# One pool of eight PSUM banks, and a table of offsets that sets the order of every step

## The chip, the cores and the metric

The kernel runs on one core of a Trainium2 chip. The core has five engines with instruction queues of their own: PE multiplies matrices, DVE, ACT and POOL work on vectors, and SP only issues DMA transfers. Each engine takes its instructions strictly in the order in which the program lists them, and waits on semaphores where an operand or a buffer is not ready. The metric is device time in microseconds, the median of several executions; less is better.

## The reference

Eight batches of attention with 8 heads of 64, 512 local and 32 global tokens, followed by a two-layer MoE block with one expert on all 4,352 tokens. Cut to what matters:

```
s_g   = scale * q_g @ concat(k_g, k_l).T          # 32 global queries see all 544 keys
s_l   = scale * q_l @ k_l.T, only |i - j| <= 32   # local queries see a band ...
s_lg  = scale * q_l @ k_g.T                       # ... and the 32 global keys
out   = softmax(...) @ concat(v_g, v_l)           # both kinds
x     = out as [4352, 512]
h     = x @ w_in                                  # 512 -> 2048
g     = h where h >= 1, 0 where h <= -1, (h + 1)^2 / 4 between
y     = g @ w_out                                 # 2048 -> 512
```

The attention inputs are float32; both weights are float64 and arrive as words of 64 bits.

## The kernel before

Every product is computed with operands that are split into two float16 halves (a high part and the rest), so one logical product is three matmuls that add up in PSUM: high by high, low by high, high by low.

**Weights** (`win_decode`, `win_scale`, `win_halves` and the same for `w_out`): a tile of 128 rows of float64 words is loaded; ACT takes the magnitude of the upper words, a shift of the lower words (DVE in all 32 tiles before) and two more DVE instructions (SCALAR_TENSOR_TENSOR) put 32-bit magnitudes and signs together; PE sums magnitudes for a scale per group of four tiles; then the tile is split into halves, in one of several ways (a string of three letters per tile names the engines; `e` goes through PE with a scaled identity `sid` in float32). There are 16 tiles of each weight.

**Attention** of batch b: `scale_k/q/v` find powers of two for the operands, `prep_k/q/v` split them, `turn` transposes a split tile of 128 by 1024 (eight blocks of 128 by 128). `att_a(b, i, pr)` handles a pair of heads for 128 queries: scores on PE, a masked maximum on DVE (the custom instruction that writes `tts_t`, and `small_nb` for the offset), exponentials on ACT (`pf`), the split of the probabilities (`pb`: the high half by a cast, the low half by a subtraction on POOL), and `turn` into `pt`. `att_b` multiplies with the values, `att_x` normalises, splits and transposes the result into `xt`. `glob_a/b` do the global queries.

**MoE** in slices of 256 tokens, called by step name `m<slice>.<f>` for the first layer (24 matmuls of 128x256; `moe1`) and `o<slice>.<tile><part>` for the second (12 of 128x512; `moe2`). After each first-layer group there are an ACT instruction, two DVE instructions of 128x512 (the ones that write `ps_h_h` and `moe_t_r`), an ACT cast and a POOL subtraction. Batch 0 gives slices 0 and 1, batch 1 gives slices 2 and 3, and so on.

**Transposes.** Before, all of batch 0 that goes through `turn` (10 tiles of k and q and 16 of probabilities) is transposed on PE with an identity, and ACT copies the PSUM tile out. Batches 1 to 7, and `xt` in all batches, go through a DMA transpose issued by SP.

**PSUM** has eight banks. Before they are four pools of fixed use: `ps_h` 3 (first layer, transposes, weight halves), `ps_o` 2 (second layer, weight sums), `ps_s` 2 (scores), `ps_x` 1 (attention output).

**What sets the order.** The program is recorded first, without being issued. `segments` groups the recorded instructions of a step by engine and finds which segment must follow which. `schedule` then plays the segments through with a table of costs (`cost`): at each moment each free engine takes, among the segments that are ready by that table and whose buffers are free, the one with the lowest `prio`. Buffers of one tag are given out nearly in recorded order: a tile may take a buffer only if the earliest tile without one keeps a free one and is less than the pool's size behind. Before, `prio` is a start time per step from the numbers in `T`; a second pass uses deadlines instead, and the better one of the two is issued. The instructions are then written out in that order, engine by engine, and nothing reorders them any more. In the profile all of them have one line (L1238), so tiles and not lines tell the steps apart.

Of the kernel before, what the change touches and what calls it, by code (L numbers as in the profile page):

```python
# [107 lines left out]

def free(ap):
    n = 1  # L110
    for d in ap.shape[1:]:
        n *= d
    return n


def cost(engine, op, a, k, outs, ins, tiles):
# [3 lines left out]
    if engine == "tensor":  # L120
        if ins and ins[0].dtype == F32:
            return 4 * n / 2.4 + 10, 0
        t = max(28.0, n / 2.4 + 2.5)
        return (t / 4 if o.shape[0] == 32 else t), 0
    if engine == "sync":
# [4 lines left out]
        return 560.0, b / (186.0 if run < 512 else 264.0 if run < 1024 else 280.0)  # L130
    if engine == "scalar":
        own = 90 if op != "activation" or mybir.dt.size(o.dtype) == 2 else 190 if "accum_out" in k else 235
# [15 lines left out]
class Segment:  # L148
    __slots__ = ("n", "engine", "calls", "t", "xfer", "after", "before", "new", "uses", "load", "step", "left", "ready", "prio", "t0", "done")


def segments(steps, tiles, prio, names):
# [5 lines left out]
    for sn, calls in enumerate(steps):  # L158
        cur = None
        for engine, op, a, k in calls:  # L160
# [3 lines left out]
            if cur is None or cur.engine != engine or engine == "sync" or fresh & {tiles[nm][0] for nm in cur.new}:  # L164
                cur = Segment()
                cur.n, cur.engine, cur.calls, cur.t, cur.xfer = len(segs), engine, [], 0.0, 0.0
# [4 lines left out]

            near = [x.tensor.name for x in sides(*cur.calls[-2])[0]] if len(cur.calls) > 1 else []
            cur.t += t + (100.0 if engine in ("vector", "scalar") and any(x.tensor.name in near for x in ins) else 0.0)
# [30 lines left out]
def schedule(segs, tiles, hop, slack, landing, ahead):  # L204
# [15 lines left out]
    for g in segs:  # L220
        if g.left == 0:
            waiting[g.engine].append(g)
    free_at = {e: 0.0 for e in engines}
    dma_free, now, events, order, landed = 0.0, 0.0, [], [], []
    while len(order) < len(segs) or events:
        went = True
        while went:
            went = False
            for e in engines:
# [3 lines left out]
                for g in waiting[e]:  # L233
                    if g.ready > now or (best is not None and (g.prio, g.n) > (best.prio, best.n)):
# [6 lines left out]
                    if any(len(slots[tag]) < len(x) + (min(x) > head[tag]) or max(x) - head[tag] >= many[tag] for tag, x in need.items()):  # L241
# [3 lines left out]
                    best = g  # L245
                if best is None:
# [3 lines left out]
                waiting[e].remove(g)  # L250
# [5 lines left out]
                free_at[e] = now + g.t  # L256
                done = now + g.t
# [17 lines left out]
        while events and events[0][0] <= now:  # L275
# [3 lines left out]
            for b in g.before:  # L279
                c = segs[b]  # L280
                wait = (hop if c.engine != g.engine else 60.0) + (slack if c.engine == "tensor" and g.engine != "tensor" else 0.0)
                c.ready = max(c.ready, now + wait)
                c.left -= 1
                if c.left == 0:
                    waiting[c.engine].append(c)
# [998 lines left out]
```

## Time and profile before

| what | us |
|---|---|
| median of 3 runs (987.35 to 989.39) | 988.6 |
| the profiled execution, its own time | 987.26 |
| its span, first to last instruction | 985.5 |
| PE busy | 904.5 |
| DVE busy | 730.4 |
| ACT busy | 601.0 |
| POOL busy | 359.5 |
| mean granted TensorE clock | 0.968 |

A busy engine in this table is one with an instruction under way; a matmul counts until its result is out, so a busy PE need not be at its peak. The span is shown in the page as 40 slices of 24.6 us, and it divides into two parts: the first quarter, in which weights are decoded while batches 0 and 1 are worked on, and the rest, in which PE is busy without a break.

### The profile page before, as it was taken

Reading aid. Unit: us, or ns where it says so; the run is one execution under the profiler, and the core shown is the slowest. Engines: PE = TensorE matmul, PEld = TensorE weight load, DVE = VectorE, ACT = ScalarE, POOL = GpSimd, SP = SyncE. Lnnn points to the kernel's source line nnn. Section 1 sums busy time; section 2 is a strip of 40 time slices with the busy share of each in tenths; the row PEclk is TensorE's granted clock in tenths of the full one; section 3 lists DMA queues with packets and bytes.
Section 4 is the critical chain, followed back from the end, with each engine's and each line's share of the span. In section 5 each row is a group of like instructions: output and inputs, shape, how many; then the busy total and the mean of one; then the engine's idle time right before and its main releaser. Section 6 shows DMA issues by size and latency. Waiting matters only on the chain.

```text
span 985.5 us, 24720 instructions
## 1 busy us (share of the span) xinstructions
PE 904.5 (92%) x9499; PEld 641.4 (65%) x9500; DVE 730.4 (74%) x1956; ACT 601.0 (61%) x1418; POOL 359.5 (36%) x383
## 2 busy tenths in 40 slices
PE   2676767898899999999999999999999999999998
PEld 1453543575667676767676777867776767676765
DVE  4799998698787879677964868787867796565432
ACT  7897768675757656656663656666676654444321
POOL 4134462254414434343433333433333343332211
PEclk9877977999899999999999999999999999999999
DMA  9842534778989659956892659766886685344101
GB/s 236 233 147 64 168 88 102 145 161 144 175 155 177 119 128 152 182 113 128 153 186 45 134 111 170 136 114 130 160 175 114 128 134 108 59 79 66 33 1 33
DMA packets 370102, 125.23 MB, mean 127 GB/s; under 512 B 346432, under 2 KB 355648, under 8 KB 369984
## 3 DMA queue, kind: packets, MB, share of 16 engines
q1 hardware_dynamic: 369984, 123.65, 63.4%
q8 instruction: 74, 1.21, 0.5%
q14 instruction: 44, 0.36, 0.1%
HBM read 43.52 MB, written 8.91 MB: 53 GB/s over the span
## 4 chain that ended last, share of the span: by engine, by line
PE 71%; DVE 16%; DMA 5%; issue 3%; ACT 2%; POOL 1%; SPq 1%; DVEq 0%; POOLq 0%; ACTq 0%
PE ps_h_h L1238 32%; PE ps_o_o L1238 30%; PE ps_s_s L1238 5%; PE ps_x_x L1238 5%; DVE tmp_tmp L1238 2%; DVE weights_w L1238 2%; DVE tts_t L1238 1%; DVE nat_nat L1238 1%; DMA xt_xt<-xn_xh 1%; DMA weights_w<-in_moe_w_in_dram 1%; DVE batch_small_ms L1238 1%; DVE ps_h_h L1238 1%; SPq L1238 1%; DVE moe_t_r L1238 1%; DVE batch_small_q L1238 1%
## 5 line engine op out<-in xcount | busy, mean ns | idle before, releaser
L1238 PE MATMUL ps_h_h<-xt_xt,weights_w 128*128 128x256 f16 (+1 forms) x3456 | 383.3, 270 | 10.2 <-ACT pt_pt L1238 6.0
L1238 PE MATMUL ps_o_o<-weights_w,hidden_g 128*128 128x512 f16 x1632 | 376.6, 381 | 2.8 <-DVE xt_xt L1238 2.8
L1238 PEld LDWEIGHTS <-weights_w 128*128 128x128 f16 x3456 | 321.7, 99 | 61.5 <-issue 15.5
L1238 PEld LDWEIGHTS <-hidden_g 128*128 128x128 f16 x1744 | 161.5, 100 | 177.6 <-issue 12.1
L1238 POOL TENSOR_TENSOR hidden_g<-moe_t_r,hidden_g 128x512 f16<-128x512 f32 (+1 forms) x144 | 165.6, 1150 | 273.2 <-ACT hidden_g L1238 267.2
L1238 POOL TENSOR_TENSOR const_pb<-pf_pf,const_pb 128x384 f16<-128x384 f32 (+1 forms) x124 | 129.3, 1045 | 276.9 <-DVE const_pb L1238 195.8
L1238 ACT ACTIVATE moe_t_r<-ps_h_h,batch_small_ms 128x512 f32<-128x512 f32 (+1 forms) x144 | 107.9, 749 | 127.2 <-PE ps_h_h L1238 119.3
L1238 DVE SCALAR_TENSOR_TENSOR ps_h_h<-ps_h_h,batch_small_ms,moe_t_r 128x512 f32<-128x512 f32 (+1 forms) x144 | 104.2, 723 | 93.0 <-ACT moe_t_r L1238 92.9
L1238 ACT ACTIVATE pf_pf<-tts_t,small_nb 128x224 f32<-128x224 f32 (+1 forms) x256 | 117.3, 459 | 91.2 <-DVE small_nb L1238 77.1
L1238 DVE CUSTOM_DVE_ANT_0 tts_t<-ps_s_s,const_mask,batch_small_q 128x192 f32<-128x192 f32 (+1 forms) x256 | 100.2, 427 | 41.1 <-PE ps_s_s L1238 39.0
L1238 ACT CAST hidden_g<-moe_t_r 128x512 f16<-128x512 f32 (+1 forms) x144 | 84.7, 588 | 61.0 <-DVE moe_t_r L1238 60.6
L1238 DVE SCALAR_TENSOR_TENSOR moe_t_r<-moe_t_r,batch_small_ms,ps_h_h 128x512 f32<-128x512 f32 (+1 forms) x144 | 103.4, 718 | 5.5
L1238 ACT ACTIVATE junk_junk<-stage_st 128x512 f16<-128x512 f32 (+1 forms) x108 | 67.5, 625 | 25.5 <-DMA stage_st<-in_v_l_dram 8.7
L1238 PE MATMUL ps_s_s<-kt_kt,qt_qa 128*128 128x32 f16 (+2 forms) x704 | 69.8, 199 | 10.4 <-DVE small_nb L1238 5.6
L1238 PEld LDWEIGHTS <-pt_pt 128*128 128x128 f16 (+1 forms) x1536 | 61.8, 98 | 15.4 <-ACT pt_pt L1238 2.5
L1238 PE MATMUL ps_x_x<-v_v,pt_pt 128*128 128x64 f16 (+1 forms) x1536 | 67.7, 194 | 0.8 <-DVE moe_t_r L1238 0.5
L1238 PE MATMUL ps_s_s<-kt_kt,qt_qb 128*128 128x32 f16 (+2 forms) x704 | 65.9, 198 | 0.0
L1238 PEld LDWEIGHTS <-qt_qb 128*128 128x128 f16 x704 | 55.4, 98 | 16.1 <-issue 13.1
L1238 PEld LDWEIGHTS <-qt_qa 128*128 128x128 f16 x704 | 59.4, 98 | 5.1 <-issue 1.5
L1238 DVE CAST const_pb<-pf_pf 128x384 f16<-128x384 f32 (+1 forms) x112 | 47.7, 431 | 10.7 <-DMA pt_pt<-const_pb 6.6
L1238 ACT ACTIVATION_READ_ACCUMULATOR pf_pf<-tts_t,small_nb 128x1 f32 x256 | 47.8, 187 | 0.0
L1238 DVE TENSOR_SCALAR small_nb<-small_nb 128x2 f32<-128x2 f32 x128 | 35.4, 277 | 4.4
(165 smaller groups left out, 900.5 us busy)
## 6 DMA issues: line engine op xcount, KB each, us to landing
stage_st<-in_q_l_dram SPq DMA_DIRECT2D x32, 256.0 KB, 4.2
weights_w<-in_moe_w_in_dram SPq DMA_DIRECT2D x32, 256.0 KB, 4.0
qt_qb<-qt_qa SPq DMA_DIRECT2D x64, 128.0 KB, 3.0
stage_st<-in_moe_w_out_dram SPq DMA_DIRECT2D x32, 256.0 KB, 3.3
out_dram<-tmp_tmp SPq DMA_DIRECT2D x30, 256.0 KB, 2.5
stage_st<-in_k_l_dram SPq DMA_DIRECT2D x24, 256.0 KB, 3.6
stage_st<-in_v_l_dram SPq DMA_DIRECT2D x21, 256.0 KB, 3.8
v_v<-v_v SPq DMA_DIRECT2D x16, 128.0 KB, 2.7
```

Source lines behind the costliest of these rows:

```text
L1238: getattr(getattr(tc.nc, engine), op)(*a, **k)
```

## The change

It has these parts.

1. **PSUM**: one pool `ps` of eight banks with one tag `b`; every PSUM tile takes any free bank. The rule on recorded order now runs over all PSUM tiles together, with a reach of eight.
2. **The planner**: `plan` makes one pass. `prio` is the deadline of a segment (`deadlines`, counted backwards over the recorded order), and to it is added an offset for the step from a new table `LATER` (323 entries, in microseconds). Segments are shorter: a chain on DVE or ACT in which one instruction reads what the one before wrote is now cut apart, so other work can be put between.
3. **The costs** of the planner: other figures for DMA, ACT and float32 matmuls; matmuls in the first 200 us cost 1.1 times as much; instructions for which `shares` holds (all of POOL but memsets, and DVE instructions with two tensors in SBUF, or a copy or tensor_scalar of SBUF) are played one after the other across the two engines.
4. **Who does what**, by strings in `T`: `turns` (batch 0's 16 probability tiles go through a DMA transpose instead of PE and ACT; k and q of batch 0 stay on PE), `shifts` (7 of 32 shifts go from DVE to POOL, where one shift is two instructions), `subs` (8 low halves of probabilities of batches 0 and 1 go from POOL to DVE), `glow` (4 low halves of slices 0 and 1 from POOL to DVE), `casts` (3 casts of batch 1 from DVE to ACT), `lows` (2 of batch 1's `att_x` subtractions from DVE to POOL), `adds` (3 of the `small_nb` additions to ACT, 3 cut in two), `splits`, `halves` (13 tiles instead of 12 go through PE's float32 identity).
5. Eight single-column maxima of `win_scale` are done as three by broadcasting.

```diff
+def shares(engine, op, a, k, tiles):
+    if engine == "gpsimd":
+        return op != "memset"
+    if engine != "vector" or op in ("memset", "reciprocal", "tensor_reduce", "tensor_tensor_reduce"):
+        return False
+    ins = {"tensor_scalar": a[1:2], "tensor_copy": a[1:2], "scalar_tensor_tensor": [a[1], a[3]] if len(a) > 3 else []}.get(op, a[1:3])
+    ins = list(ins) or [k["in0"], k["in1"]]
+    held = [x for x in ins if is_ap(x) and not tiles.get(x.tensor.name, (0, 0, 1))[2]]
+    return len(held) > 1 or (op in ("tensor_scalar", "tensor_copy") and len(held) == 1 and free(held[0]) > 1)
...
-                free_at[e] = now + g.t
-                done = now + g.t
+                done, slow = now, SLOW if e == "tensor" and now < 2.0e5 else 1.0
+                for t, shared in g.parts:
+                    if shared:
+                        pair = done = max(pair - LEAD, done) + t
+                    else:
+                        done += t * slow
+                free_at[e] = done
...
 def plan(steps, tiles, prio, names, hop, slack, landing, ahead):
     segs = segments(steps, tiles, prio, names)
-    best = None
-    for n in range(PASSES):
-        order, taken, end = schedule(segs, tiles, hop, slack, landing, ahead)
-        if best is None or end < best[2]:
-            best = order, taken, end, [g.t0 for g in segs]
-        deadlines(segs, [g.n for g in segs] if n == 0 else order, hop, slack, landing)
-    order, taken, end, t0 = best
-    for g, t in zip(segs, t0):
-        g.t0 = t
+    if T["late"]:
+        deadlines(segs, [g.n for g in segs], hop, slack, landing)
+    for g in segs:
+        g.prio += LATER.get(g.step, 0.0) * (1.0e3 if T["late"] else 1.0)
+    order, taken, _ = schedule(segs, tiles, hop, slack, landing, ahead)
     return order, segs, taken
...
-    ps_h = pool("ps_h", 3, space=PSUM)
-    ps_o = pool("ps_o", 2, space=PSUM)
-    ps_s = pool("ps_s", 2, space=PSUM)
-    ps_x = pool("ps_x", 1, space=PSUM)
+    ps = pool("ps", 8, space=PSUM)
...
-    def turn(b, o, i):
-        if b:
+    def turn(who, o, i):
+        if who == "d":
             dma_t(o, i)
             return
         n = i.shape[0]
-        t = ps_h.tile([P, 8, P], F16, tag="h", name="turn")
+        t = ps.tile([P, 8, P], F16, tag="b", name="turn")
         for c in range(8):
             nc.tensor.transpose(t[:, c, :n], i[:, c * P:(c + 1) * P], ident[:n, :n])
-        nc.scalar.copy(o, t[:, :, :n])
+        (nc.scalar.copy if who == "a" else nc.vector.tensor_copy)(o, t[:, :, :n])
...
-        (nc.vector.tensor_copy if b else nc.scalar.copy)(pb[:, 0, :, :w], pf[:, :, :w])
-        nc.gpsimd.tensor_tensor(pb[:, 1, :, :w], pf[:, :, :w], pb[:, 0, :, :w], op=ALU.subtract)
+        (nc.scalar.copy if of("casts", b, 4 * i + pr, 16, "v") == "a" else nc.vector.tensor_copy)(pb[:, 0, :, :w], pf[:, :, :w])
+        (nc.vector if of("subs", b, 4 * i + pr, 16, "p") == "v" else nc.gpsimd).tensor_tensor(pb[:, 1, :, :w], pf[:, :, :w], pb[:, 0, :, :w], op=ALU.subtract)
         pt = ptp.tile([P, 2, 2, 2, P], F16, tag="pt", name=f"pt{b}_{i}_{pr}")
-        turn(b, pt.rearrange("p j u c k -> p (j u c) k"), pb.rearrange("p j u c -> p (j u c)"))
+        turn(of("turns", b, 10 + 4 * i + pr, 30, "d"), pt.rearrange("p j u c k -> p (j u c) k"), pb.rearrange("p j u c -> p (j u c)"))
...
+LATER = {"Lk00": -3, "Lk01": -33.7, "Lk02": 1.2, "Lk10": -99.1, "Lk11": 66.5, "Lk12": 98.5, "Lk20": -95.5, "Lk21": -87.9,
...
+T = dict(late=1, lk0=1.06, lq0=1.76, lv0=30, sk=12, sq=14, adds="vvvvvv1vvvvvavvvvvvvavv1vvvvv1av",
+         subs="pppppppppppvvvpppppvpvpvvppppvpp", glow="pppvpppvpppvpvpp",
+         turns="aaaaaaaaaadddddddddddddddddddddddddddddddddddddddddddddddddd", casts="aaaaaaaaaaaaaaaavvavvvavvvvvvavv",
...
+         shifts="pppvpvvpvvvvvvvvvvvvvvvvvpvvvpvv", splits="vvvvvvvvvvvpvvvpvvvpvppp", att=1.35, s0=60, s1=100, s2=254.09,
```

Three places in the order show what moved.

**DVE, the first instructions.** Tiles `weights_w` are weight tiles, `tmp_tmp` their magnitudes, `small_amk` and `batch_small_q` the scales of k and q. Before:

```order
L1238 TENSOR_REDUCE small_amk_91<-small_amk_91 128x1
L1238 TENSOR_SCALAR small_asx_93<-small_amk_91 128x1
L1238 COPY small_amk_91<-ps_s_s_97 128x1
L1238 TENSOR_SCALAR small_amk_91<-small_amk_91 128x1 x2
L1238 TENSOR_SCALAR batch_small_sk_98<-small_amk_91 128x1
L1238 RECIPROCAL batch_small_sk_98<-batch_small_sk_98 128x1
L1238 TENSOR_SCALAR batch_small_q_0_102<-batch_small_q_0_102 128x2 x3
```

With the change:

```order
L1278 SCALAR_TENSOR_TENSOR tmp_tmp_90<-tmp_tmp_90,weights_w_0_66 128x512
L1278 SCALAR_TENSOR_TENSOR weights_w_0_66<-weights_w_0_66,tmp_tmp_90 128x512
L1278 SCALAR_TENSOR_TENSOR tmp_tmp_95<-tmp_tmp_95,weights_w_0_67 128x512
L1278 SCALAR_TENSOR_TENSOR weights_w_0_67<-weights_w_0_67,tmp_tmp_95 128x512
L1278 SCALAR_TENSOR_TENSOR tmp_tmp_96<-tmp_tmp_96,weights_w_0_68 128x512
L1278 TENSOR_SCALAR weights_w_0_69<-weights_w_0_69 128x512
L1278 SCALAR_TENSOR_TENSOR weights_w_0_68<-weights_w_0_68,tmp_tmp_96 128x512
```

The decoding of the first four weight tiles now stands ahead of the scales of k and q, and the shifts of the first three of them are on POOL.

**ACT before, SP with the change: the probability tiles of batch 0.** `pf` are exponentials, `hidden_g` and `const_pb` the split probabilities, `pt` their transposes. On ACT before:

```order
L1238 ACTIVATE pf_pf_139,small_sum_138<-tts_t_153,small_nb_152 128x192 x2
L1238 CAST hidden_g_140<-pf_pf_139 128x2x192
L1238 ACTIVATE hidden_g_109<-stage_st_116,batch_small_q_0_102 128x8x64
L1238 COPY pt_pt_147<-ps_h_h_105 128x1024
L1238 ACTIVATE pf_pf_146,small_sum_138<-tts_t_137,small_nb_136 128x192 x2
L1238 CAST hidden_g_141<-pf_pf_146 128x2x192
L1238 ACTIVATE tmp_tmp_120<-weights_w_0_72 128x512
L1238 COPY pt_pt_154<-ps_h_h_105 128x1024
```

On SP with the change, where before only loads and copies stood:

```order
L1280 DMA stage_st_87<-in_moe_w_out_dram 128x512 x2
L1278 DMA_TRANSPOSE pt_pt_135<-const_pb_0_61 128x8x128
L1278 DMA_TRANSPOSE pt_pt_144<-hidden_g_133 128x8x128
L1278 DMA_TRANSPOSE pt_pt_138<-const_pb_0_62 128x8x128
L1278 DMA v_v_0_156<-v_v_149 32x1024
L1278 DMA v_v_159<-v_v_149 32x1024
L1278 DMA v_v_1_158<-v_v_149 32x1024
L1280 DMA stage_st_126<-in_moe_w_out_dram 128x512 x2
```

The 16 ACT copies and the 128 PE transposes ahead of them are gone from their queues, and 16 transposes stand in SP's queue between loads of `w_out`.

**DVE, the passage from slice 0 to slice 1.** `xt_xt_89` and `xt_xt_139` hold the output of slice 0 here; a pair that writes a PSUM tile and then `moe_t_r` belongs to a first-layer group of slice 1. Before:

```order
L1238 SCALAR_TENSOR_TENSOR nat_nat_190<-stage_st_85,batch_small_sk_186,nat_nat_190 128x8x64
L1238 SCALAR_TENSOR_TENSOR xt_xt_89<-ps_o_o_115,batch_small_ms_170,xt_xt_89 128x512
L1238 SCALAR_TENSOR_TENSOR xt_xt_89<-ps_o_o_143,batch_small_ms_170,xt_xt_89 128x512
L1238 SCALAR_TENSOR_TENSOR xt_xt_89<-ps_o_o_115,batch_small_ms_170,xt_xt_89 128x512
L1238 SCALAR_TENSOR_TENSOR nat_nat_190<-stage_st_0_87,batch_small_sk_186,nat_nat_190 32x8x64
L1238 SCALAR_TENSOR_TENSOR nat_nat_192<-stage_st_86,batch_small_q_1_198,nat_nat_192 128x8x64
L1238 SCALAR_TENSOR_TENSOR ps_h_h_101<-ps_h_h_101,batch_small_ms_170,moe_t_r_171 128x512
L1238 SCALAR_TENSOR_TENSOR moe_t_r_171<-moe_t_r_171,batch_small_ms_170,ps_h_h_101 128x512
```

With the change:

```order
L1278 SCALAR_TENSOR_TENSOR ps_b_102<-ps_b_102,batch_small_ms_171,moe_t_r_173 128x512
L1278 SCALAR_TENSOR_TENSOR nat_nat_195<-stage_st_0_88,batch_small_sk_192,nat_nat_195 32x8x64
L1278 SCALAR_TENSOR_TENSOR moe_t_r_173<-moe_t_r_173,batch_small_ms_171,ps_b_102 128x512
L1278 SCALAR_TENSOR_TENSOR ps_b_94<-ps_b_94,batch_small_ms_171,moe_t_r_172 128x512
L1278 SCALAR_TENSOR_TENSOR moe_t_r_172<-moe_t_r_172,batch_small_ms_171,ps_b_94 128x512
L1278 SCALAR_TENSOR_TENSOR nat_nat_193<-stage_st_86,batch_small_q_1_199,nat_nat_193 128x8x64
L1278 SCALAR_TENSOR_TENSOR xt_xt_139<-ps_b_117,batch_small_ms_171,xt_xt_139 128x512
```

Before, slice 0 was finished on DVE before slice 1 began; now two groups of slice 1 stand ahead of slice 0's last parts.

More of the change, by code (lines that the diff above doesn't have):

```diff
@@ L148 @@
 class Segment:
-    __slots__ = ("n", "engine", "calls", "t", "xfer", "after", "before", "new", "uses", "load", "step", "left", "ready", "prio", "t0", "done")
+    __slots__ = ("n", "engine", "calls", "t", "xfer", "after", "before", "new", "uses", "load", "step", "parts", "left", "ready", "prio", "t0", "done")
 def segments(steps, tiles, prio, names):
@@ L170, in segments @@
             cur.calls.append((op, a, k))
-            near = [x.tensor.name for x in sides(*cur.calls[-2])[0]] if len(cur.calls) > 1 else []
-            cur.t += t + (100.0 if engine in ("vector", "scalar") and any(x.tensor.name in near for x in ins) else 0.0)
+            cur.t += t
+            cur.parts.append((t, shares(engine, op, a, k, tiles)))
             cur.xfer += x
@@ L221, in schedule @@
         if g.left == 0:
-            waiting[g.engine].append(g)
+            bisect.insort(waiting[g.engine], (g.prio, g.n, g))
     free_at = {e: 0.0 for e in engines}
-    dma_free, now, events, order, landed = 0.0, 0.0, [], [], []
+    dma_free, pair, now, events, order, landed = 0.0, 0.0, 0.0, [], [], []
     while len(order) < len(segs) or events:
@@ L232, in schedule @@
                 best = None
-                for g in waiting[e]:
-                    if g.ready > now or (best is not None and (g.prio, g.n) > (best.prio, best.n)):
+                for at, (_, _, g) in enumerate(waiting[e]):
+                    if g.ready > now:
                         continue
@@ L280, in schedule @@
                 c = segs[b]
-                wait = (hop if c.engine != g.engine else 60.0) + (slack if c.engine == "tensor" and g.engine != "tensor" else 0.0)
+                wait = (hop if c.engine != g.engine else OWN) + (slack if c.engine == "tensor" and g.engine != "tensor" else 0.0)
                 c.ready = max(c.ready, now + wait)
@@ L302, in deadlines @@
             c = segs[b]
-            wait = (hop if c.engine != g.engine else 60.0) + (slack if c.engine == "tensor" and g.engine != "tensor" else 0.0)
+            wait = (hop if c.engine != g.engine else OWN) + (slack if c.engine == "tensor" and g.engine != "tensor" else 0.0)
             x = min(x, late[b] - wait - took)
@@ L858, in att_a @@
                                            op0=ALU.add, op1=ALU.min, accum_out=nb[:, u:u + 1])
[L859 removed]
+        who = of("adds", b, 4 * i + pr, 16, "v")
+        if who == "a":
+            nc.scalar.activation(nb2, nb, AF.Identity, bias=logp[:, 0:1])
+        else:
+            for u in range(2) if who == "1" else (slice(0, 2),):
+                x = slice(u, u + 1) if who == "1" else u
+                nc.vector.tensor_scalar(nb2[:, x], nb[:, x], LOGP, None, op0=ALU.add)
         pf = pfp.tile([P, 2, 224], F32, tag="pf", name=f"pf{b}_{i}_{pr}")
@@ L1028, in moe2 @@
         if part == gs[0]:
-            OP[key, t] = ps_o.tile([P, DM], F32, tag="o", name=f"o{key}_{t}_{part}")
+            OP[key, t] = ps.tile([P, DM], F32, tag="b", name=f"o{key}_{t}_{part}")
         o = OP[key, t]
```

130 lines of the change are left out of this document (71 added, 59 removed), and 41 rows, old and new, of the table LATER.

## The prediction

> **What bounds the kernel now.** I began with the slices of the page:
>
> ```profile
> PE   2676767898899999999999999999999999999998
> DVE  4799998698787879677964868787867796565432
> PEclk9877977999899999999999999999999999999999
> ```
>
> PE is short of work only in the first ten to twelve slices; there DVE is the full engine. To find the border I took the chain of waits (start, length, what; us) near the end of that stretch:
>
> ```profile
> 163.10 5.28 PE ps_o_o L1238 x12
> ...
> 185.09 3.32 DMA xt_xt<-xn_xh
> 188.46 7.08 PE ps_h_h L1238 x48
> ...
> 249.51 3.30 DMA xt_xt<-xn_xh
> 252.86 3.33 PE ps_h_h L1238 x24
> ```
>
> At 252.86 us PE starts the first group of slice 2 (`m2.0`). Then I asked for busy times by stage (length, then PE, PEld, DVE, ACT, POOL with instruction counts, granted clock, DMA share, GB/s):
>
> ```profile
> 0.00:50.00 50.00, 22.62 (x193) 15.95 (x194) 31.50 (x93) 39.65 (x85) 15.71 (x39) 0.92 0.96 235
> 50.00:150.00 100.00, 71.52 (x707) 49.69 (x707) 93.79 (x217) 76.79 (x151) 46.78 (x45) 0.83 0.40 113
> 150.00:200.00 50.00, 39.48 (x316) 23.81 (x317) 36.29 (x86) 35.83 (x80) 14.56 (x17) 0.86 0.62 129
> 200.00:252.86 52.86, 45.34 (x577) 31.69 (x575) 47.80 (x153) 33.92 (x100) 25.56 (x25) 0.95 0.80 156
> ...
> 252.86:985.50 732.64, 725.53 (x7709) 520.24 (x7708) 521.03 (x1410) 414.85 (x1007) 256.88 (x258) 1.00 0.64 119
> ```
>
> The last row is the key. From `m2.0` to the end PE is busy 725.53 of 732.64 us at full clock, on 7709 matmuls. In the order of the changed kernel I counted the matmuls from its first `m2.0` on: 7709 again, of the same shapes. So the second part, B, costs 732.6 us as before; it can gain 7.1 us at most. **The whole change is decided by when `m2.0` starts.**
>
> Ahead of that (part A, 252.86 us) DVE is busy 209.4 us and idle 43.5: 18.5 in 0 to 50, 6.2 in 50 to 150, 13.7 in 150 to 200, 5.1 after. Its busy time is not all work:
>
> ```profile
> 120.00 0.98 DVE L1238 TENSOR_SCALAR batch_small_ms<-const_tm,batch_small_sv 128x2 f32<-128x2 f32 x1
> 121.88 1.90 DVE L1238 TENSOR_SCALAR batch_small_ms<-batch_small_ms 128x2 f32<-128x2 f32 x2
> 124.93 0.17 DVE L1238 TENSOR_SCALAR batch_small_ms<-batch_small_ms 128x2 f32<-128x2 f32 x1
> 129.32 0.42 DVE L1238 TENSOR_SCALAR stage_st<-stage_st 128x512 int32<-128x512 int32 x1
> 129.85 0.69 DVE L1238 SCALAR_TENSOR_TENSOR tmp_tmp<-tmp_tmp,stage_st 128x512 int32<-128x512 int32 x1
> 135.00 1.46 DVE L1238 SCALAR_TENSOR_TENSOR tmp_tmp<-tmp_tmp,stage_st 128x512 int32<-128x512 int32 x1
> ```
>
> ```profile
> 122.47 1.15 POOL L1238 TENSOR_TENSOR weights_w<-tmp_tmp,weights_w 128x512 f16<-128x512 f32 x1
> 135.87 1.60 POOL L1238 TENSOR_TENSOR hidden_g<-moe_t_r,hidden_g 128x512 f16<-128x512 f32 x1
> ```
>
> An instruction on two columns takes 0.17 us or nearly 1; the same decode instruction takes 0.69 or 1.46. The long ones coincide with POOL at work. Means of groups in 37.5 to 250 us (count, busy us, mean ns) show how much this costs:
>
> ```profile
> L1238 DVE SCALAR_TENSOR_TENSOR tmp_tmp<-tmp_tmp,stage_st 128x512 int32<-128x512 int32 x16 | 12.6, 788 | 2.3 <-ACT tmp_tmp L1238 0.7
> L1238 DVE SCALAR_TENSOR_TENSOR weights_w<-stage_st,tmp_tmp 128x512 int32<-128x512 int32 x16 | 12.5, 782 | 0.6
> L1238 DVE SCALAR_TENSOR_TENSOR weights_w<-weights_w,tmp_tmp 128x512 int32<-128x512 int32 x9 | 9.6, 1072 | 0.3
> L1238 DVE TENSOR_SCALAR stage_st<-stage_st 128x512 int32<-128x512 int32 x16 | 8.7, 542 | 0.0
> L1238 DVE TENSOR_SCALAR small_nb<-small_nb 128x2 f32<-128x2 f32 x29 | 8.3, 288 | 1.0
> ```
>
> Against 0.69, 0.42 and 0.17 alone the excess is 1.6 + 1.5 + 3.4 + 2.0 + 3.4 = 11.9 us in these five groups; with the two-column instructions above some 14. I call this the lock.
>
> **The change part by part.** Rows for what is moved:
>
> ```profile
> L1238 PE MATMUL ps_h_h<-const_ident,const_pb 128*128 128x128 f16 x96 | 8.6, 229 | 8.9 <-DVE moe_t_r L1238 3.4 <-POOL const_pb L1238 2.4 <-ACT const_pb L1238 1.2
> L1238 PE MATMUL ps_h_h<-const_ident,hidden_g 128*128 128x128 f16 x96 | 11.1, 291 | 4.7 <-DVE hidden_g L1238 2.3 <-ACT weights_w L1238 1.9 <-ACT pt_pt L1238 0.4
> L1238 ACT COPY pt_pt<-ps_h_h 128x1024 f16<-128x1024 f16 x16 | 16.0, 1002 | 0.3 <-PE ps_h_h L1238 0.2
> L1238 POOL TENSOR_SCALAR tmp_tmp<-weights_w,const_wo 128x512 f32<-128x512 f32 x8 | 5.7, 722 | 4.0 <-DVE const_wo L1238 3.8
> L1238 POOL TENSOR_SCALAR tmp_tmp<-stage_st,batch_small_sv 128x512 f32<-128x512 f32 x2 | 2.3, 1170 | 0.0
> L1238 DVE TENSOR_TENSOR xn_xh<-xn_xn,xn_xh 128x512 f16<-128x512 f32 x2 | 1.4, 679 | 0.0
> L1238 DVE CAST const_pb<-pf_pf 128x448 f16<-128x448 f32 x8 | 5.2, 672 | 0.4 <-DMA pt_pt<-const_pb 0.4
> ```
>
> *PE.* The 16 probability tiles leave: 96 matmuls of the first row and 32 of the second, 8.6 + 11.1/3 = 12.3 us of busy PE. They lie in A, where PE idles 73.9 us; worth nothing by themselves. One more weight tile through the float32 identity costs some 2 us, hidden there too. *ACT* loses 16.0 us of copies and gains three casts and three additions, some 2. *DVE*: seven shifts leave (7 x 0.42 = -2.9), 12 subtractions come; no such row exists, the nearest is the subtraction into `xn_xh` (12 x 0.68 = +8.2), two of those leave (-1.4), three casts leave (-1.0 to -2.0, by 0.35 to 0.67), five maxima leave and one split more goes to POOL (-1.5). Sum +1; bounds -1 and +3. *POOL* gains 14 passes of 0.72 to 1.17 (10 to 16 us; the shift itself isn't in the trace) and loses 12 subtractions of about 1.1: even.
>
> So no engine has much less to do in A except ACT and PE, which are not the full ones. What remains is DVE's idle time and its lock, and both go by the order.
>
> *0 to 50 us.* The longest wait of DVE:
>
> ```profile
> DVE small_amk L1238 <- ACT junk_junk L1238: 10.9, 1, 10.9
> ```
>
> Its first work comes at 12 us, behind POOL's memsets (8 us) and ACT's squares of k. Now the first work is a weight tile: memsets, then two POOL passes, 9.4 to 10.2 us. After that the loads bound it: DMA was busy 0.96 of this stretch at 235 GB/s, and the same tiles are needed. I take -4 (bounds 0 and -7).
>
> *50 to 150.* DVE is 94% busy; ACT's lost copies and the cut chains can fill a part of the 6.2: -2 (0 to -4).
>
> *150 to 200.* The chain shows why DVE starves: PE does the second layer of slice 0 (12 matmuls in 5.28 us, at half clock), then waits for `xt` of slice 1, and DVE has no first-layer group to work on. Now two of slice 1's groups stand ahead of slice 0's last parts, so this gap closes for the most part. 13.7 idle: -9 (0 to -12). PE bounds it: it is busy 84.8 of the last 102.9 us of A, so no more than 18 can go there.
>
> *200 to 252.86.* -1 (0 to -3).
>
> *Lock.* The total of POOL stays, so only placing helps; the planner now plays DVE's two-tensor instructions and POOL's one after the other. Of 14 I take -6 (+6 to -10).
>
> *PSUM pool.* Eight banks for all replaces three, two, two and one. PE waits for ACT or DVE to empty a bank are a few us in A and inside the stretches above; I add nothing.
>
> *DMA transposes.* Sixteen more, in a stretch with DMA share 0.40:
>
> ```profile
> pt_pt<-const_pb SPq DMA_TRANSPOSE x112, 3.3
> SPq L1240 <- DVE weights_w L1238: 53.9, 17, 16.5
> ```
>
> 3.3 us from issue to landing instead of about 2 for eight matmuls and a copy. With three `pt` buffers in flight, 1.1 us a tile, this is no more than the DVE time per pair of heads (two reductions of 0.4 and small ones), so 0.
>
> Sum: +1 - 4 - 2 - 9 - 1 - 6 = -21 us. A becomes 232, the span 985.5 - 21 = 964.5, the execution 987.26 - 21 = 966.3, and as the median lies 1.3 above the profiled execution, 967.6. Best bounds together: -37, or 951, and 944 with B's 7.1.
>
> A rule of the Trainium skill speaks against the change: GPSIMD Engine Reference, section Key points, says that POOL shares its SBUF interfaces with VectorE and that DVE instructions with two SBUF inputs (or in a two-port mode) contend with it. The rows 0.69 and 1.46 agree. By it the 12 subtractions that come to DVE are of the kind that contends; the rival "lock" below gives what that would make of the time. A second one, TensorE: Matmul & The Clock Gate, part 1, says that PE falls to half clock after an idle window of about 3.4 us. PEclk of 0.83 with PE 72% busy agrees; with 12 us less for PE in A the clock could sink further, and an estimate of 4 us more on the path would give 971.
>
> **The rivals.**
>
> *Transposes hold SP (slower).* SP issues in order; a transpose that waits for POOL's low half holds every load behind it, and the `w_out` loads already wait 53.9 us for free buffers. For it: the order above puts them between `w_out` loads. Against: DMA share 0.40. If each of 16 holds the next load by 2 us and DVE's decode waits for it, +32 - 21 = +11: 999. It decides once DVE's `stage_st` instructions wait for DMA. 15%.
>
> *Lock grows.* Each of 12 subtractions meets one POOL instruction of 1 us, and placing helps nothing: +12 + 6 on the sum, -3: 985 at worst, 980 where half of it comes. 12%.
>
> *Nothing reaches the path.* An order made for other durations than the chip's gives DVE's idle time back in other places: 988. 5%.
>
> *A near its floor.* The best bounds come together: DVE idle only at the start, lock halved: 944 to 954. For it: the gaps are all waits for order, not for work. Against: DMA is full until 50 us, PE nearly so after 150. 20%.
>
> **How the numbers follow.** The forecast, -21 with its own range 955 to 979, has 48%. Faster by over 0.2% (2 us, about what a measurement of this kernel tells from no change) are forecast, floor and most of the grown lock: 80%. Within 0.2%: 5%. Slower: 15%. The range is 944 to 990: it leaves out a little of the floor (7%) and the slower case (13%).
>
> **What would show it.** Right: `m2.0` starts at 225 to 240 us; B remains 730 to 733 us; DVE idle in 150 to 200 falls to about 5; first DVE work at 10 us; 16 fewer ACT copies; the decode groups' means nearer 0.70. Wrong: PE idle in B (then the order of deadlines fails where PE was full); DVE waiting for DMA `stage_st` between 60 and 150 (SP held); `weights_w` decode means of over 1 us (lock); or A shorter with PE waiting after 250 for `xt`.

## The result and the profile after

The changed kernel takes 965.32 us (median of 4 executions, 964.09 to 968.07) against 988.65 us before (987.35 to 989.39): ratio 0.977, 95% interval 0.975 to 0.979. The profiled execution took 965.34 us, of which the span is 963.6 us. The forecast was 967.6.

The slices of the changed kernel's page, of the same three rows as before:

```profile
PE   1863997988999999999999999999999999999997
DVE  3889997888878886679565885879757985564332
PEclk9776898998999999999999999999999999999999
```

PE is now full from the eleventh slice on, before from the twelfth. The border between the two parts, `m2.0`, stands in the chain of waits:

```profile
231.01 0.33 DVE tts_t L1278
231.36 13.66 PE ps_b L1278 x154
```

The busy time by stage of the kernel before, cut at its `m2.0` (length, then PE, PEld, DVE, ACT, POOL with their counts, granted clock, DMA share, GB/s):

```profile
0.00:252.86 252.86, 178.96 (x1790) 121.14 (x1792) 209.38 (x547) 186.20 (x412) 102.61 (x125) 0.88 0.64 149
252.86:985.50 732.64, 725.53 (x7709) 520.24 (x7708) 521.03 (x1410) 414.85 (x1007) 256.88 (x258) 1.00 0.64 119
```

and of the changed one:

```profile
0.00:231.36 231.36, 163.18 (x1666) 110.70 (x1667) 191.78 (x543) 168.37 (x396) 116.37 (x129) 0.87 0.79 180
231.36:963.60 732.24, 725.70 (x7709) 521.56 (x7709) 511.36 (x1409) 411.34 (x1013) 258.13 (x260) 1.00 0.66 120
...
0.00:50.00 50.00, 23.66 (x140) 13.74 (x141) 30.96 (x78) 33.47 (x62) 22.66 (x41) 0.90 0.96 250
50.00:150.00 100.00, 72.71 (x770) 49.65 (x770) 94.39 (x258) 80.14 (x193) 60.75 (x55) 0.83 0.65 159
150.00:200.00 50.00, 41.13 (x369) 29.13 (x365) 40.26 (x111) 35.26 (x82) 23.09 (x25) 0.93 0.85 168
```

B, from `m2.0` to the end, is the same to 0.4 us. A, ahead of it, is 21.5 us shorter, of the 21.9 by which the two profiled executions differ. But DVE's **idle** time in A, from which the prediction took most of the gain, went only from 43.5 to 39.6 us. What fell is DVE's **busy** time, 209.4 to 191.8 us, on nearly the same number of instructions (547 and 543). Either DVE's instructions became shorter, or they began to overlap: the busy time of a stage counts a moment in which two records lie over each other once.

To tell these apart I went through every DVE record of A in order of time. Their lengths add up to L. A record that begins before the one ahead of it has ended gives an overlap (O); one that begins up to 0.3 us after that end gives a short gap (S); a later one a long gap (G). L - O + S + G is the time at which A ends, to within half a microsecond.

| us | L | O (pairs) | S (pairs) | G | `m2.0` at |
|---|---|---|---|---|---|
| before | 232.8 | 23.1 (290) | 11.6 (241) | 31.7 | 252.9 |
| changed | 230.3 | 38.2 (483) | 2.9 (40) | 36.5 | 231.4 |
| difference | -2.5 | -15.1 | -8.7 | +4.8 | -21.5 |

The instructions are as long as before. They follow each other faster: some 200 pairs with a short gap between them became pairs that overlap, and this is worth 15.1 + 8.7 = 23.8 us. The trace shows what separates the two kinds. In the timeline of the kernel before, DVE's scales of the first-layer output (`batch_small_ms`; start, length, what):

```profile
124.93 0.17 DVE L1238 TENSOR_SCALAR batch_small_ms<-batch_small_ms 128x2 f32<-128x2 f32 x1
...
125.76 0.15 DVE L1238 RECIPROCAL batch_small_ms<-batch_small_ms 128x2 f32<-128x2 f32 x1
125.94 0.90 DVE L1238 TENSOR_TENSOR batch_small_ms<-batch_small_ms 128x2 f32<-128x2 f32 x1
126.88 1.07 DVE L1238 TENSOR_TENSOR batch_small_ms<-batch_small_ms,const_t2o 128x2 f32<-128x2 f32 x1
127.88 0.75 DVE L1238 SCALAR_TENSOR_TENSOR ps_h_h<-ps_h_h,batch_small_ms,moe_t_r 128x512 f32<-128x512 f32 x1
128.66 0.75 DVE L1238 SCALAR_TENSOR_TENSOR moe_t_r<-moe_t_r,batch_small_ms,ps_h_h 128x512 f32<-128x512 f32 x1
```

The ones at 125.94, 126.88 and 128.66 read what the one ahead of them wrote, and start just after that has ended (125.76 + 0.15 = 125.91, next start 125.94; 127.88 + 0.75 = 128.63, next 128.66). The one at 127.88 starts 0.07 us before the end of the one ahead. In the changed kernel the same scales stand between those of `w_out`:

```profile
100.38 0.15 DVE L1278 TENSOR_SCALAR const_wo<-small_womx 128x1 int32<-128x1 int32 x1
100.45 0.15 DVE L1278 RECIPROCAL batch_small_ms<-batch_small_ms 128x2 f32<-128x2 f32 x1
100.52 0.20 DVE L1278 SCALAR_TENSOR_TENSOR batch_small_ms<-const_wt,batch_small_sv,batch_small_ms 128x2 f32<-128x2 f32 x1
100.64 0.15 DVE L1278 TENSOR_SCALAR const_wo<-const_wo 128x1 f32<-128x1 f32 x1
100.70 0.23 DVE L1278 TENSOR_SCALAR batch_small_ms<-batch_small_ms 128x2 f32<-128x2 f32 x2
100.84 0.15 DVE L1278 RECIPROCAL const_wo<-const_wo 128x1 f32<-128x1 f32 x1
100.91 0.13 DVE L1278 TENSOR_SCALAR const_wo<-const_wo 128x1 f32<-128x1 f32 x1
```

Here an instruction mostly has another between itself and its input, and starts some 80 ns before its predecessor's end. By the names that they write and read, 272 of A's pairs followed a predecessor whose tile they read before, 93 do now. (The names do not tell whether it is the part just written that is read: 65 of these 93 overlap too.) In the kernel before, the median pair of the first kind has a gap of 34 ns, of the other an overlap of 81: 115 ns a pair. I call this the **cadence**. The lines of the change that do it are four in `segments`: a piece of the plan now ends wherever an instruction of VectorE or ScalarE reads what the one ahead of it wrote, so that the planner may put another in between; before, the two were one piece with 100 ns added.

A sentence of the Trainium skill bears on this. "VectorE: DVE Perf Modes", section "The DRAIN you can't avoid", says of eight copies in a row that a semaphore after each costs nothing extra over one after the last, since the next operation waits for the pipe to empty in any case; it adds that one which is not held starts earlier. For an instruction that reads its predecessor's result the pairs here disagree, with 34 ns after the end against 81 before. If that had held for these pairs too, parting them would have brought nothing of the 23.8 us.

### The profile page after: what moved, and what is told of

Same layout as the page of the kernel before. It is cut to its first block, busy times and chain, and to the rows that moved or that the text cites. A ratio compares the mean times of both kernels' runs of the same rounds, so it can differ in the third digit from the quotient of the medians.

```text
span 963.6 us, 24479 instructions
## 1 busy us (share of the span) xinstructions
PE 888.9 (92%) x9375; PEld 632.3 (66%) x9375; DVE 703.1 (73%) x1951; ACT 579.7 (60%) x1408; POOL 374.5 (39%) x389
## 4 chain that ended last, share of the span: by engine, by line
PE 78%; DVE 7%; ACT 6%; DMA 4%; issue 3%; POOL 1%; SPq 1%; ACTq 0%; DVEq 0%; POOLq 0%
PE ps_b L1278 78%; DVE tmp_tmp L1278 1%; DMA stage_st<-in_k_l_dram 1%; DVE weights_w L1278 1%; ACT junk_junk L1278 1%; ACT weights_w L1278 1%; ACT pf_pf L1278 1%; ACT tmp_tmp L1278 1%; DVE tts_t L1278 1%; DMA weights_w<-in_moe_w_in_dram 1%; DMA pt_pt<-const_pb 1%; DVE stage_st L1278 1%; ACT hidden_g L1278 1%; POOL hidden_g L1278 0%; SPq L1278 0%
## 5 line engine op out<-in xcount | busy, mean ns | idle before, releaser
L1278 PE MATMUL ps_b<-xt_xt,weights_w 128*128 128x256 f16 (+1 forms) x3456 | 384.0, 269 | 1.8 <-DMA xt_xt<-xn_xh 1.2
L1278 PE MATMUL ps_b<-weights_w,hidden_g 128*128 128x512 f16 x1632 | 372.5, 379 | 1.4 <-DVE xn_xn L1278 1.4
L1278 POOL TENSOR_TENSOR const_pb<-pf_pf,const_pb 128x448 f16<-128x448 f32 (+1 forms) x116 | 120.5, 1040 | 236.8 <-DVE const_pb L1278 121.7
L1278 DVE SCALAR_TENSOR_TENSOR ps_b<-ps_b,batch_small_ms,moe_t_r 128x512 f32<-128x512 f32 (+1 forms) x144 | 104.1, 724 | 101.4 <-ACT moe_t_r L1278 101.1
L1278 ACT ACTIVATE moe_t_r<-ps_b,batch_small_ms 128x512 f32<-128x512 f32 (+1 forms) x144 | 107.7, 748 | 104.1 <-PE ps_b L1278 98.9
L1278 ACT ACTIVATE pf_pf<-tts_t,small_nb 128x192 f32<-128x192 f32 (+1 forms) x256 | 117.0, 458 | 85.7 <-DVE small_nb L1278 69.2
L1278 DVE CUSTOM_DVE_ANT_0 tts_t<-ps_b,const_mask,batch_small_q 128x192 f32<-128x192 f32 (+1 forms) x256 | 99.0, 428 | 23.0 <-PE ps_b L1278 22.3
L1278 DVE SCALAR_TENSOR_TENSOR moe_t_r<-moe_t_r,batch_small_ms,ps_b 128x512 f32<-128x512 f32 (+1 forms) x144 | 102.3, 712 | 2.6
L1278 PE MATMUL ps_b<-v_v,pt_pt 128*128 128x64 f16 (+1 forms) x1536 | 69.2, 195 | 12.6 <-DMA pt_pt<-const_pb 9.0
L1278 PEld LDWEIGHTS <-pt_pt 128*128 128x128 f16 (+1 forms) x1536 | 62.7, 99 | 25.9 <-DMA pt_pt<-const_pb 13.7
L1278 PE MATMUL ps_b<-kt_kt,qt_qa 128*128 128x128 f16 (+2 forms) x704 | 68.6, 198 | 0.8 <-DVE small_amv L1278 0.6
L1278 PE MATMUL ps_b<-tmp_tmp,const_ones 128*128 128x128 bf16 (+1 forms) x76 | 15.0, 307 | 36.6 <-DVE tmp_tmp L1278 36.5
```

What stands on the lines that cost most here:

```text
L1278: getattr(getattr(tc.nc, engine), op)(*a, **k)
```

## Is it the cadence? One part alone, and that part undone

Theory A: the cadence makes the gain. Theory B: the prediction's (the order of the long work, gaps, the lock). In the cuts of the edits below, comments stand for lines left out. Each run was timed beside the kernel before, whose median was 987.3 to 988.3 us there against 988.65 above, so that a microsecond between two runs tells nothing.

**The cut alone** (`before_cut`), in the kernel before, planned again:

```diff
+            near = [... for x in sides(*cur.calls[-1])[0]] if cur and cur.engine == engine in ("vector", "scalar") else []
             if (cur is None or ... 
+                    or any(x.tensor.name in near for x in ins)):
-            cur.t += t + (100.0 if engine in ("vector", "scalar") and any(... in near ...) else 0.0)
+            cur.t += t
-            wait = (hop if c.engine != g.engine else 60.0) + ...
+            wait = (hop if c.engine != g.engine else 100.0) + ...
```

> The kernel before with one part of the change alone: its planner makes a new piece wherever an instruction of VectorE or ScalarE reads what the one ahead of it wrote, and asks for 100 ns between such pieces, so that another instruction can be put between the two. Strings, pools, shifts and the two passes of the planner stay. Theory A (cadence): on VectorE an instruction that reads its predecessor's result starts 34 ns after it has ended, any other 81 ns before, and the gain of the change is the 179 pairs of this kind that went from the stretch ahead of m2.0 (272 before, 93 after; 179 x 0.115 = 20.6 us). The order has some 200 such pairs less here too: 965 to 973. Theory B (the prediction: gaps, lock and the order of the long work; cut chains are worth 2 us at most): 984 to 990.

985.47 us (ratio 0.998, 0.997 to 0.999). By time this is theory B. By the records it is neither: O rose to 35.1, S fell to 4.6 us, so that the cadence gained 19.0 us, and long gaps rose from 31.7 to 47.9. In the profiled execution, at 988.43 the slowest of the ten, B took 5.7 us more too. The cut gives DVE the time, and the new plan loses it by waiting.

**The cut undone in the order alone** (`after_glued`): the changed kernel's plan is made, and then each DVE piece that reads the DVE piece ahead of it in its chain is moved up right behind it where the data allow:

```diff
+            # for each VectorE piece g at place i, the next piece h that reads what g wrote, at place j
+                if not between & h.after and not last:
+                    order.insert(i + 1, order.pop(j))
```

> The changed kernel with its order kept, except that on VectorE a piece that reads its predecessor's result is moved up to stand right behind it again wherever the data allow: 218 such pairs ahead of m2.0 in the order, where the changed kernel has 30. Nothing else is moved, the work of each engine is the same. Theory A (cadence): 188 x 0.115 = +21.6 us, 985 to 989, with m2.0 at 251 to 255. Theory B (order of the long work): 964 to 969.

982.60 us (981.52 to 985.23), 17.3 us above the changed kernel. Its stages:

```profile
0.00:247.76 247.76, 168.34 (x1666) 112.17 (x1666) 202.08 (x540) 168.86 (x395) 117.42 (x129) 0.84 0.73 167
247.76:983.50 735.74, 727.05 (x7709) 522.03 (x7709) 527.06 (x1412) 412.63 (x1013) 257.48 (x260) 1.00 0.66 120
```

`m2.0` comes 16.4 us later, and L, O, S, G say why: 226.7, 24.4, 10.2, 35.4. Cadence +21.1, lengths -3.6, long gaps -1.1. Theory A gave 21.6 for the cadence, and 985 to 989 for the time, which came out lower. It did not see that the lengths get shorter when DVE is slower. B grew too, by 3.5 us in this execution, which was the slowest of its seven.

**The cut alone with the order kept** (`before_woven`): the kernel before, its own plan, strings and pools; only afterwards the next ready DVE piece is moved between two that depend on each other.

```diff
+    order = [x for n in order for x in at[n]]        # the old plan's pieces, each cut into its parts
+    return woven(order, parts, tiles, taken, hop), parts, taken
...
+            # p, q: neighbours on VectorE, q reads p; z: one of the next 10 pieces, its inputs long done
+            order.insert(j, order.pop(x))
```

> The kernel before with its own plan, strings and pools; only afterwards its pieces are cut where VectorE reads its predecessor's result, and the next ready VectorE piece is moved in between. Counted in the order ahead of m2.0 some 190 dependent pairs less. This is the change's one suspected cause alone, with the order of the long work kept. Theory A (cadence, 0.115 us a pair, and long gaps stay as they are since the order stays): up to 190 x 0.115 = 22 us, so 967 to 974. Theory C (what the cadence frees comes back as longer gaps unless the order is made anew, as in the run before_cut, where 14.3 us of VectorE time left and the gaps of over 300 ns grew by 16.2): 980 to 988.

977.35 us (975.70 to 979.20), ratio 0.989 (0.987 to 0.991): 10.7 us, nearly half of the result, with nothing else of the change.

```profile
0.00:242.71 242.71, 177.82 (x1792) 120.51 (x1793) 201.71 (x557) 185.34 (x412) 107.83 (x125) 0.90 0.69 155
```

L 237.0, O 34.6, S 3.7, G 37.1: the cadence gave 19.4 us, as expected, and 4.2 went back in longer instructions and 5.4 in long gaps. So the truth lies between A and C: most of the cadence (19.0 and 19.4 of 23.8 us) is there whenever the pairs are parted, and a part of it returns unless the rest of the order fits. The changed kernel's `m2.0` is another 11.3 us earlier. By the same sums 6.7 of these are shorter instructions (237.0 to 230.3), 4.4 cadence and 0.6 long gaps; what makes the instructions shorter, the order or the work moved between engines, no run separates.

## The table of offsets

**No table** (`after_nolater`) and **a table off by up to 1 us** (`after_jitter`):

```diff
-        g.prio += LATER.get(g.step, 0.0) * (1.0e3 if T["late"] else 1.0)
+        g.prio += 0.0 * (1.0e3 if T["late"] else 1.0)
```

```diff
+        g.prio += 1.0e3 * ((names.index(g.step) * 7919 % 101) / 50.0 - 1.0)
         g.prio += LATER.get(g.step, 0.0) * (1.0e3 if T["late"] else 1.0)
```

> The changed kernel without its table of offsets: each piece goes by its deadline alone. Theory C (cadence is kept, the gaps come back): VectorE's dependent pairs ahead of m2.0 stay below 70, its gaps over 300 ns go to 50 us or more, 980 to 995. If the table is worth nothing: 964 to 969.

> The changed kernel with every offset of its table moved by a fixed number between -1 and +1 us and planned again: a change without meaning. It says how much of the 25 and 17 us that four pools and PE's transposes cost was only that the table no longer fitted the plan. If the table fits like a key (theory C): 975 to 985, with VectorE's gaps over 300 ns ahead of m2.0 at 45 to 50 instead of 36.5 us and the cadence kept. If the offsets are broad: 964 to 969.

986.11 us (983.68 to 990.94) and 984.86 us (981.22 to 991.68). Both keep the cadence (O 38.9 and 36.5, S 3.1 and 2.8 us) and both have G at 47, where the changed kernel has 36.5; L is 238.1 and 233.6 instead of 230.3. Offsets of up to 298 us, moved by at most 1, are worth no more than none: the table fits one plan like a key. The profiled execution of the jittered kernel, 989.9 us, is among its slowest; B took 741.64 us there, with PE busy 729.44 of them:

```profile
0.00:246.46 246.46, 162.48 (x1668) 110.76 (x1669) 196.87 (x536) 168.56 (x395) 115.41 (x131) 0.89 0.75 167
246.46:988.10 741.64, 729.44 (x7709) 523.61 (x7707) 510.06 (x1416) 414.73 (x1015) 257.47 (x258) 0.99 0.65 119
```

**The same disturbance of the kernel before** (`before_jitter`):

```diff
+    prio = [p + (known.index(n) * 7919 % 101) / 50.0 - 1.0 for p, n in zip(prio, names)]
```

> The kernel before with every time of its steps moved by a fixed number between -1 and +1 us and planned again, as the run after_jitter did with the changed kernel. If its numbers fit its plan as closely as the changed kernel's table does (theory C): 995 to 1010, and then a replanned kernel with cut chains (985.5) is to be held against this one and not against 988. If its plan is broad: 986 to 991, and all of the 19.5 us that the changed kernel lost by the same disturbance is what its table adds.

988.59 us (987.31 to 990.54), ratio 1.000 (0.999 to 1.002). L 234.2, O 23.0, S 11.7, G 31.7: nothing moves. But this run can't say that the plan before is broad, for the disturbance did not reach it. In the two traces all 1956 instructions of DVE, 1417 of ACT and 383 of POOL stand in the same order, on the same tiles. The planner before makes a second pass by deadlines, which it counts back over the recorded order and not from the start times that were moved, and it is that pass's order that was issued both times. How the old plan would bear a real disturbance stays open, and a like comparison is missing. What is shown: the new planner without its table, or with the table disturbed, lies at 985 to 986, some 2 to 4 us below before, and the table as it is brings 20 us more. With the pairs glued the keyed plan has 17 us less; with the pairs parted the old plan has 10.7 more (`before_woven`). The two shares do not add up to a sum: the plans with the cadence whose order does not fit (`before_cut`, `after_nolater`, `after_jitter`) have 10 to 16 us more of long gaps.

## The pool, the transposes and the engines' strings

**Four pools, planned again** (`after_fourpools`), and **the changed order kept, then put into four pools** (`after_pools_kept`):

```diff
-    ps = pool("ps", 8, space=PSUM)
+    ps_h = pool("ps_h", 3, space=PSUM)
+    ps_o = pool("ps_o", 2, space=PSUM)
+    ps_s = pool("ps_s", 2, space=PSUM)
+    ps_x = pool("ps_x", 1, space=PSUM)
```

```diff
+    one = {nm: ("ps" if t[2] else t[0], 8 if t[2] else t[1], t[2]) for nm, t in tiles.items()}
+    order, _, _ = schedule(segs, one, hop, slack, landing, ahead)
+    order, taken = kept(order, segs, tiles)      # same order, a piece waits until its pool has a bank
```

> The changed kernel with four PSUM pools of three, two, two and one bank in place of one of eight; planned again. The prediction put the pool at 0: 964 to 969. The rival: with eight banks for all, PE and DVE wait less for each other ahead of m2.0; then 972 to 980.

> The changed kernel's order, made with one pool, then its tiles put into four PSUM pools of three, two, two and one bank with the order kept as near as the banks allow (the PE pieces shift by at most 8 places). If the pool is worth nothing by itself, as predicted: 964 to 970, and the 990.8 of the replanned kernel was the plan. If the pool carries the gain: 980 to 992, with PE waiting for VectorE and ScalarE ahead of m2.0.

990.76 us (989.84 to 991.76) and 1055.63 us, both outside every range of their expectations. The first is 25.4 us above the changed kernel, but 19.5 of that a disturbance without meaning costs as well. The other 6 us need not be the pool's: other replanned kernels differ among themselves by 3.7 us (982.41 to 986.11). The second shows that the order does use the eight banks freely:

```profile
0.00:277.16 277.16, 179.29 (x1666) 118.34 (x1666) 192.00 (x545) 169.87 (x396) 117.10 (x129) 0.79 0.65 150
277.16:1053.20 776.04, 739.26 (x7714) 527.25 (x7711) 512.83 (x1409) 413.45 (x1012) 253.90 (x260) 0.98 0.61 113
```

With the banks tied to kinds of tiles, A takes 45.8 us more and B 43.8, and L, O and S stay (229.2, 36.8, 2.7): all of A's loss is long gaps, 82.3 us. What a plan tuned for four pools would reach was not tried, so the pool's own worth stays open; that *this* plan needs it is shown.

**The probability tiles of batch 0 back on PE and ACT** (`after_turns`), planned again:

```diff
-         turns="aaaaaaaaaadddddddddddddddd...
+         turns="aaaaaaaaaaaaaaaaaaaaaaaaaa...
```

> The changed kernel with the 16 probability tiles of batch 0 turned on PE and copied by ScalarE again instead of by DMA; planned again. The prediction put the 12.3 us of PE and 16 us of ScalarE at nothing and the transposes at 0: 963 to 969. The rival that they do reach the path: 970 to 980. The rival that the transposes in SP's queue cost: 955 to 962.

982.41 us (979.34 to 989.77), above every range of the expectation: 17.1 above the changed kernel, and no more than the meaningless disturbance costs (19.5). It says nothing for or against the transposes; only their waits can be read, below.

Three further kernels keep the changed plan instruction by instruction and only move work to another engine at the same place, so that no table has to fit.

**Subtractions back on POOL** (`after_subs_kept`). The edit sets the string `subs` to POOL; this moves the eight subtractions of probability tiles. The four of first-layer outputs go by another string and stayed, so the expectation's twelve should read eight.

```diff
+        T["subs"] = "p" * 32        # between the planning and the second pass
```

> The changed kernel's plan, kept instruction by instruction, with the 12 subtractions of the low halves of batches 0 and 1 that it gives to VectorE back on POOL, at the same places. The prediction priced them at 8.2 us on VectorE and POOL's side at even. If VectorE's busy time is what counts: 957 to 961. If POOL's longer passes (1.0 to 1.6 us) come late for the transposes or stretch VectorE's instructions: 966 to 975.

966.28 us (964.74 to 969.86), no different from the changed kernel's. Their prices in the changed kernel, by groups:

```profile
L1278 DVE TENSOR_TENSOR const_pb<-pf_pf,const_pb 128x448 f16<-128x448 f32 x4 | 2.8, 694 | 0.1
L1278 DVE TENSOR_TENSOR hidden_g<-moe_t_r,hidden_g 128x512 f16<-128x512 f32 x4 | 2.7, 677 | 0.0
L1278 DVE TENSOR_TENSOR const_pb<-pf_pf,const_pb 128x384 f16<-128x384 f32 x3 | 2.0, 657 | 0.0
```

DVE was rid of 4.8 us of such work ahead of `m2.0`; L fell by 0.8 only, long gaps grew by 3.2, and `m2.0` came 2.7 us later in the profiled execution. Work taken from the fullest engine at a kept order did not shorten anything here.

**Shifts on DVE**: the first three (`after_first_v`), and all seven (`after_shifts_kept`).

```diff
+        if who == "q":
+            nc.vector.tensor_scalar(lo, lo, 29, None, op0=ALU.logical_shift_right)
...
+        T["shifts"] = T["shifts"].replace("p", "q", 3)      # all seven: without the 3
```

> The changed kernel's plan, kept, with the shifts of the first three weight tiles on VectorE (0.42 us each) in place of two passes on POOL (2.7 to 3.0 us a tile). VectorE waits 9.64 us for the first of them. The prediction's term for the start: VectorE begins some 5 us earlier and the stretch ahead of m2.0 loses up to 4 us: 961 to 963. If the loads bound this stretch (DMA share 0.96), the wait moves a few instructions on: 964 to 967.

> The changed kernel's plan, kept, with all seven shifts that it gives to POOL on VectorE. POOL loses 19.5 us of passes, VectorE gains 7 x 0.42 = 2.9 and the pairs 0.8. If VectorE's own work counts: 967 to 970. If POOL's work stretches VectorE's by more than that (the lock, as the prediction feared): 958 to 964.

966.89 us (965.51 to 967.53) and 967.10 us (962.21 to 968.80): neither can be told from the changed kernel. In the first, DVE begins its decoding at 7.9 us, before POOL is done with its memsets, and the waits move on. Its longest waits in A:

```profile
DVE weights_w L1284 <- DMA weights_w<-in_moe_w_in_dram: 7.7, 3, 6.8
DVE small_amk L1284 <- ACT junk_junk L1284: 6.1, 2, 4.7
```

where the changed kernel has

```profile
DVE tmp_tmp L1278 <- POOL weights_w L1278: 9.6, 1, 9.6
```

`m2.0` is at 232.1 against 231.4. The start then waits for a weight load and for ACT, as the second branch of the expectation had it for the loads. With all seven on DVE, POOL has 18.9 us less in A and `m2.0` came 2.3 us earlier in the profiled execution (229.0), which took 962.21; the three others took 966.28 to 968.80. No version's median beat the changed kernel's.

## Why the prediction was right, step by step

*The border.* Right. B is 732.24 us (forecast 730 to 733) on the same 7709 matmuls, and DVE's busy time in B fell by 9.7 us (521.03 to 511.36) without any effect. "The whole change is decided by when `m2.0` starts" held for the change. It is no law for every plan: B took 731.5 to 734.0 us in eight of the fourteen profiled executions, 3.5 to 10.6 us more than in the changed kernel in five, and 43.8 more with the tied banks.

*The sum.* `m2.0` at 231.36 for a forecast of 232, -21.5 for -21. **The total was right and its composition wrong.** The step that failed is "what remains is DVE's idle time and its lock, and both go by the order". Of the 43.5 us that I read as idle, 11.6 were short gaps behind instructions that DVE itself had just finished; no order of the long work closes those, parting the pairs does. And 15.1 us came out of the busy time, which I had taken as fixed except for the lock. "Cut chains" stood in the sum with a share of 2 us at 50 to 150; the pairs that they part were worth 23.8. That the sum still met the time is luck: 16 us were forecast from idle time that shrank by 4, and the cadence, which was all but left out, gave about as much as all terms together.

*0 to 50, -4.* Wrong: DVE's first work comes at 10.7 us instead of 12, as foreseen, but its idle time there went from 18.5 to 19.0, and starting it earlier still changes nothing (`after_first_v`).

*50 to 150, -2.* Idle 6.2 to 5.6: -0.6.

*150 to 200, -9.* Idle 13.7 to 9.7: -4.0, though the same 50 us hold later work now. A part of that gap was closed; in all of A long gaps grew by 4.8.

*200 to 252.86, -1.* Idle 5.1 before; 5.2 now in the shorter stretch from 200 to 231.36.

*Lock, -6.* Mis-sized: L fell by 2.5 in all, with about the same work in it. Decoding of `w_out` became longer, not nearer 0.70 (groups of all of A):

```profile
L1278 DVE SCALAR_TENSOR_TENSOR tmp_tmp<-tmp_tmp,stage_st 128x512 int32<-128x512 int32 x16 | 14.8, 933 | 0.3 <-POOL stage_st L1278 0.3
L1278 DVE SCALAR_TENSOR_TENSOR weights_w<-stage_st,tmp_tmp 128x512 int32<-128x512 int32 x16 | 13.8, 874 | 0.0
L1278 DVE SCALAR_TENSOR_TENSOR weights_w<-weights_w,tmp_tmp 128x512 int32<-128x512 int32 x15 | 11.9, 803 | 0.1
L1278 DVE TENSOR_SCALAR stage_st<-stage_st 128x512 int32<-128x512 int32 x14 | 9.5, 687 | 0.0
L1278 DVE TENSOR_SCALAR batch_small_ms<-batch_small_ms 128x2 f32<-128x2 f32 x10 | 2.3, 252 | 0.0
```

933 and 874 ns against 788 and 782, 687 against 542; the two-column scales and the decoding of `w_in` became shorter (`batch_small_ms` from 4.0 to 2.3 us in all; `weights_w` from `weights_w` from 920 ns to 803). That the plan has a part in L shows in the kernel without the table, where L is 238.1.

*DVE's work, +1.* Right to what can be read: eleven subtractions lie in A, 7.5 us at 0.66 to 0.69, where I took twelve at 0.68.

*POOL, even.* Mis-sized: the shift's second pass takes 2.06 us, not 0.72 to 1.17,

```profile
L1278 POOL TENSOR_SCALAR weights_w<-weights_w 128x512 int32<-128x512 f32 x5 | 10.3, 2057 | 0.4
L1278 POOL TENSOR_SCALAR weights_w<-weights_w 128x512 f32<-128x512 uint16 x5 | 3.9, 784 | 1.3 <-DMA weights_w<-in_moe_w_in_dram 0.9
```

so the seven cost 19.5 us and POOL is busy 116.4 us in A instead of 102.6. It costs no time that the runs can tell (`after_shifts_kept`).

*Transposes, 0, and the rival that they hold SP.* No sign of the rival: DVE has no wait for `stage_st` by DMA among its longest in A, and SP's wait for free weight buffers is shorter than the 53.9 us before:

```profile
SPq L1280 <- DVE weights_w L1278: 18.0, 9, 5.8
```

Nor are the transposes without waits: PE waits for them in A about as long as it waited for ACT's copies before. The two rows, before and changed:

```profile
PE ps_h_h L1238 <- ACT pt_pt L1238: 8.2, 7, 2.2
PE ps_b L1278 <- DMA pt_pt<-const_pb: 9.0, 4, 4.4
```

*PSUM pool, 0.* This order takes 90 us more without it (`after_pools_kept`); what the pool is worth to an order made for four stays open.

*PE's clock.* The 4 us of the prediction's estimate did not come: granted 0.88 in A before, 0.87 now, with 15.8 us less of busy PE.

*The other rivals.* "Lock grows" came true in the decode groups and not in the sum. "Nothing reaches the path" is what the new planner does without its table (985 to 986). "Near its floor" asked for DVE idle only at the start and half the lock; neither came. (Half of the grown lock is +9 by the prediction's own terms, so 976 and not its 980.)

*The signs.* `m2.0`, B, DVE's first work (10.7) and the 16 ACT copies came as named. DVE's idle time in 150 to 200 (9.7 for about 5) and the decode means did not, and these two were the signs of the terms for gaps and lock. No sign of being wrong was seen.

## What to carry over

An engine that a windowed view shows 94% busy can still have nearly 10% to give: add up the lengths of its instructions, and look at whether neighbours overlap or follow with a small gap. Where one reads what the one ahead wrote, put a third between them (here 0.115 us a pair, 10.7 us of 988 by a rule of some forty lines on a finished plan, with nothing planned again). And before a part of a tuned plan is priced by taking it out and planning again, disturb the plan without meaning: here that alone cost 19.5 us, more than most parts. Then see in the trace that the order did change: in `before_jitter` it had not.

## What the runs showed of the chip that was not expected

Two DVE instructions overlap in the records by some 80 ns (median 81 in the kernel before) unless the second reads the first's result; then it starts 34 ns after the end. I had read the busy share as work.

DVE's lengths and its cadence pull against each other: parting the pairs at a kept order made the instructions 4.2 us longer in all (232.8 to 237.0), gluing them 3.6 us shorter (230.3 to 226.7). That DVE, when it pauses less, meets POOL's instructions more often would fit; no run here separates it from the shift in time.

On POOL a TENSOR_SCALAR on 128 x 512 takes 0.78 us from uint16 to float32 (a multiplication and an addition) and 2.06 us from float32 to int32 (an addition and a subtraction). Which of the two differences makes it longer was not tried.
